# Attention and two feed-forward nets on one core: the first net's activation as one Mish instruction, weight decoding without Exp, and a planner that prices table loads

## The chip, the cores and the metric

One Trainium2 chip, one of its cores. The metric is device time in microseconds (us) of one execution; a lower one is better. Engines are named as in the profile: PE is TensorE, DVE is VectorE, ACT is ScalarE, POOL is GpSimd, SP is SyncE, whose queue issues most of the transfers.

## The reference

Three stages follow each other; inputs come as 64-bit floats.

```python
# attention: 4 batches, 8 heads, 576 positions, 64 wide
out_d  = softmax(q_d k_d^T / 8) v_d      # q_d, k_d, v_d: means over 4 neighbouring positions
local  = softmax(mask(q k^T / 8)) v      # mask: only |i - j| < 4
x = repeat(out_d, 4) + local             # [2304, 512] after joining heads
# first net, 2048 wide
h = x @ w_in
g = h * tanh(log(1 + exp(h)))            # Mish
x = g @ w_out
# second net, 1024 wide
h = x @ w3
s = h * softmax(h)
y = layernorm(s) * g_ln @ w4             # [2304, 512]
```

## The kernel before

**Work.** The 2304 tokens are 18 units of 128, in five blocks of 4, 3, 3, 4 and 4 units. `local` makes one unit's local attention: scores (line 336), Exp (line 357, or eight of them for later units), transposes (382), values (400), and the sum with the coarse part, written as two parts, high and low, into the block's x (421, 423). `coarse` makes one half of a batch's coarse attention: scores (477), six Exp with sums (491), transposes (511) with copies (514), values (525) and a copy (529). Block 0's attention comes first; that of later blocks runs between the matmuls of the first net. The tiles ku, qu and vu of later units have one buffer each.

**First net.** It runs in 80 slots, 16 for each block; the order of the segments is ten slots of block 0, sixteen of block 1, the last six of block 0, then blocks 2, 3 and 4. A slot is one chunk f of 128 of the 2048 columns of w_in for all tokens of a block (512 or 384). `chunk_in` makes h in twelve matmuls (line 632: four parts of the depth, three products of high and low parts) and then g:

```python
act: e = Exp(h)                     # line 640
dve: e = min(e, E_MAX)              # line 641
act: e = Square(e + 1)              # line 642
act: e = Ln(0.5 * e + 0.5)          # line 644
act: e = Exp(-e)                    # line 645
dve: e = (e - 1) * h                # line 646, that is -Mish(h)
act: g_high = copy(e)               # line 648
dve: g_low  = e - g_high            # line 649
```

`chunk_out` adds g's product with w_out into y (line 660, twelve matmuls), `block_end` copies y out (lines 674 on DVE, 677 on ACT) and turns the sign. h has two PSUM buffers; h is read from line 640 to line 646. The attention's tiles share the other PSUM tag, "at", with two buffers.

**Weights.** `decode` takes the bytes of the 64-bit weights apart: DVE builds the mantissa (543), ACT makes two factors from the top byte, read once as signed and once as unsigned, with Exp at a step of 16 ln 2 (545, 547), and DVE subtracts and multiplies (549, 550). `split` makes a high and a low part (553, 554).

**Second net.** `tile_in` takes 128 tokens through w3 (line 701), softmax, layer norm (Ln and Exp for the root, 742 and 743) and transposes (765); `tile_out` multiplies with w4 (782).

**Order.** Nothing runs in the order of the code. Each call of `op` puts down an engine, a cost, a wanted time ("want", in slots), its buffers and a function. `Plan.run` then plays the engines through with these costs: an engine that is free takes, of its operations that are ready and find buffers, the one with the smallest want. The order that comes out is the program. LAG is the delay that the plan adds from one engine to another; NEXT says for four slots how early and how far apart the next block's units and coarse halves are wanted; NDT, CND and CLOAD stretch the steps within them; G2LAG is the want of a tile's second product in the second net. Before the first operation, line 232 loads the table "natural_log_exp_and_others", and all Exp, Ln and Square of the kernel work with it.

Of the kernel before, what the change touches and what calls it, by code (L numbers as in the profile page):

```python
# [10 lines left out]
I32 = mybir.dt.int32  # L11
I8 = mybir.dt.int8
# [44 lines left out]


STEP = 11.090354888959125

E_MAX = 485165195.0
# [16 lines left out]
class Plan:  # L78
# [6 lines left out]
    def op(self, eng, cost, want, fn, r=(), w=(), lag=None, after=(), join=False):  # L85
# [20 lines left out]
        self.ops.append((eng, cost, want, fn, deps, list(bufs.values()), lag))  # L106
        return n

    def run(self):
# [17 lines left out]
        now, dma = 0.0, 0.0  # L127
        while len(order) < len(ops):
            for eng, queue in ready.items():
                while at[eng] <= now:  # L130
                    back, pick = [], None
                    while queue:
                        item = heapq.heappop(queue)
                        need = {}
                        for b in ops[item[1]][5]:
                            if b.tag is not None and id(b) not in held:
                                need[b.tag] = need.get(b.tag, 0) + 1
                                free.setdefault(b.tag, b.bufs)
                        if all(free[t] >= k for t, k in need.items()):
                            pick = item[1]  # L140
                            break
                        back.append(item)
                    for item in back:
                        heapq.heappush(queue, item)
                    if pick is None:
                        break
                    _, cost, _, _, _, bufs, lag = ops[pick]
# [46 lines left out]
def kernel(  # L194
# [37 lines left out]
    nc.scalar.preload_act_table_set("natural_log_exp_and_others")  # L232
# [21 lines left out]
    def act(cost, want, fn, r, w, after=()):  # L254
        return op("act", cost, want, fn, r, w, after=after)
# [31 lines left out]
    def local(u, t0, dt, gate_x=()):  # L287
# [66 lines left out]
        if u < MERGE:  # L354
            dve(dve_us(8 * KW), t0 + 0.2 * dt, lambda: nc.vector.tensor_tensor(
                heads(), heads(), nm()[:, :8].unsqueeze(2).to_broadcast([UQ, 8, KW]), op=ALU.add), [nm], [sm])
            act(act_us(8 * KW), t0 + 0.25 * dt, lambda: nc.scalar.activation(heads(), heads(), AF.Exp), [], [sm])
            dve(dve_us(8 * KW), t0 + 0.3 * dt, lambda: nc.vector.tensor_reduce(
                su()[:, :8], heads(), axis=AX.X, op=ALU.add), [sm], [su])
        else:  # L360
            for h0 in range(0, 8, 4):
                def expo(h0=h0):
                    for i in range(h0, h0 + 4):
                        nc.scalar.activation(heads()[:, i, :], heads()[:, i, :], AF.Exp, bias=nm()[:, i:i + 1],
                                             accum_out=su()[:, i:i + 1])

                act(4 * 0.32, t0 + 0.25 * dt, expo, [nm], [sm, su])
# [36 lines left out]
        passed["x", u] = pe(1.2 if early else 0.7, t0 + 0.7 * dt, values, [v, at] + ups, o + [xf], after=gate_x)  # L404
# [20 lines left out]
    def coarse(b, g2, t0, dt):  # L425
# [61 lines left out]
        for h2 in range(2):  # L487
            def expo(h2=h2):
# [5 lines left out]
            act(3 * 0.36, t0 + 0.3 * dt, expo, [nm, sc[h2]], [sm, su])  # L494
# [10 lines left out]
        for h2 in range(2):  # L505
            for k in range(2):
                tp = P("h" if early else "at")

                def flip(h2=h2, k=k, tp=tp):
                    for i in range(3):  # L510
                        nc.tensor.transpose(tp()[:72, 128 * i:128 * i + 128], sm()[:, h2, i, 72 * k:72 * k + 72], ident())  # L511

                def take(h2=h2, k=k, tp=tp):
# [3 lines left out]
                pe(0.6 if early else 0.3, t0 + 0.5 * dt, flip, [sm, ident], [tp, at])  # L517
# [15 lines left out]
    def decode(x, part, raw, n, want):  # L533
# [5 lines left out]
        plus = lambda: fb()[:, :n]  # L539
        minus = lambda: bytes_(BF16)[:, :n]  # L540
# [44 lines left out]
    g1_op = {}  # L585
    wi = {}
# [36 lines left out]
    def chunk_in(s, i, f, N):  # L623
# [4 lines left out]
        def g1():  # L628
# [24 lines left out]
    def chunk_out(s, f, fs, N, g, y):  # L653
        w = wo[f // 2]
        for d2 in range(2):
# [7 lines left out]
            pe(6 * (N + 32) / 2400, s + 1.7, g2, [w, g], [y[d2]])  # L663

    def block_end(i, s, N, y, more):
        t0 = starts[i]
        tags = (("ys", 2), ("raw", 2)) if i < NB - 1 else (("vu", 1), ("atT", 1))
        for d2 in range(2):
            ys = S([128, 2, NMAX], *tags[d2])
            for d in range(2):  # L670
                src = lambda d=d, d2=d2: y[d2]()[:, d, :N]
                dst = lambda d=d, ys=ys: ys()[:, d, :N]
                if d2:
                    dve(dve_us(N), s + 1.7, lambda src=src, dst=dst: nc.vector.tensor_scalar(
                        dst(), src(), -1.0, None, op0=ALU.mult), [y[d2]], [ys])
                else:
                    act(act_us(N), s + 1.7, lambda src=src, dst=dst: nc.scalar.activation(  # L677
                        dst(), src(), AF.Copy, scale=-1.0), [y[d2]], [ys])
# [4 lines left out]
    def tile_in(t, s):  # L683
# [11 lines left out]
        for m in range(2):  # L695
# [8 lines left out]
            pe(12 * 0.216, s, g1, [x] + [w3t[c, m][0] for c in range(4)], [hs[m if first else 0]], after=[g1_op[16 * NB - 1]] if first else ())  # L704
# [3 lines left out]
        if first:  # L708
# [5 lines left out]
            for m in range(2):  # L714
                act(act_us(512, 0.2), s + 0.2, lambda m=m: nc.scalar.activation(
                    e()[:, m], part(m), AF.Exp, bias=nm()[:, 0:1], accum_out=su()[:, 1 + m:2 + m]), [hs[m], nm], [e, su])
            dve(0.08, s + 0.3, lambda: nc.vector.tensor_tensor(
                su()[:, 0:1], su()[:, 1:2], su()[:, 2:3], op=ALU.add), [], [su])
        else:
# [3 lines left out]
                e(), hs[0](), AF.Exp, bias=nm()[:, 0:1], accum_out=su()[:, 0:1]), hs + [nm], [e, su])  # L723
# [29 lines left out]
        act(0.35, s + 0.3, root, [], [r])  # L753
# [5 lines left out]
        for m in range(2):  # L759
# [7 lines left out]
            pe(0.43, s + 0.9, flip, [e, ident], [tp])  # L767
# [6 lines left out]
    def tile_out(t, s, ln):  # L774
# [10 lines left out]
        pe(24 * 0.216, s + G2LAG, g2, [ln] + [w4t[k][0] for k in range(8)], [o])  # L785
# [13 lines left out]
    dve(0.1, -99, lambda: nc.vector.memset(ones()[:, 2:3], -64 * STEP), [], [ones])  # L799
    dve(0.1, -99, lambda: nc.vector.memset(ones()[:, 3:4], -192 * STEP), [], [ones])  # L800
# [49 lines left out]
    for k in range(8):  # L850
        second_split(k, 16 * NB - 16 + 2 * k + 2)
    for t in range(NTI):
# [72 lines left out]
```

## Time and profile before

| | |
|---|---|
| time, median of 3 runs | 742.58 us (742.24 to 742.71) |
| profiled execution, span from first to last instruction | 740.9 us |
| median less that span | 1.68 us |
| PE busy | 701.5 us, 95% |
| DVE busy | 473.3 us, 64% |
| ACT busy | 440.0 us, 59% |
| table loads | one, 1283 ns |

The page gives no other time of its own for the profiled execution than its span; the runs' times hold what lies around it as well. A busy PE counts a matmul from its start to its modelled end, and matmuls overlap, so "busy" says little on how dense the work is; the distance from one start to the next says more. The mean of 373 ns for a matmul of 512 columns on the page is such an overlapped duration.

### The profile page before, as it was taken

To read this page: it belongs to the slowest core of one execution; us is meant where nothing else is said; L and a number is where in the kernel's file an instruction comes from. 1 tells how busy PE (TensorE), PEld (TensorE's weight loads), DVE (VectorE), ACT (ScalarE), POOL (GpSimd) and SP (SyncE) were. 2 spreads that over 40 slices of the span, in tenths; PEclk is the share of its full clock that TensorE was granted. 3 is DMA by queue.
4 is the path that set the end of the run, shared out by engine and by line. 5 is a ranking of instruction groups with operands and counts; after the bars stand their busy time and mean duration, and the time that the engine had idled before them with its cause. 6 is when DMAs were issued, how large, how long until landed. Compare 5 with 4: busy or idle time off the path is not lost.

```text
span 740.9 us, 14030 instructions
## 1 busy us (share of the span) xinstructions
PE 701.5 (95%) x5720; PEld 593.3 (80%) x5720; DVE 473.3 (64%) x995; ACT 440.0 (59%) x845; POOL 33.5 (5%) x44
## 2 busy tenths in 40 slices
PE   1577999999999999999999999999999999999998
PEld 1365787899988899998888888888788888888886
DVE  4788886685854465756565545534698767667660
ACT  1458996798976677877667677756443332323321
POOL 2000101011011011000000000000000000000000
PEclk9756999999999999999999999999999999999999
DMA  8977834664353076635333123111210111010101
GB/s 240 265 264 216 248 107 96 210 146 130 114 117 85 13 162 188 161 109 179 100 112 107 63 106 116 59 56 43 82 46 30 43 42 58 30 57 29 43 28 44
DMA packets 56449, 80.48 MB, mean 109 GB/s; under 512 B 4160, under 2 KB 35392, under 8 KB 56384
## 3 DMA queue, kind: packets, MB, share of 16 engines
q1 hardware_dynamic: 52128, 72.25, 30.4%
q0 software_dynamic: 4256, 7.33, 6.2%
q8 instruction: 45, 0.74, 0.4%
q14 instruction: 20, 0.16, 0.1%
HBM read 64.88 MB, written 14.68 MB: 107 GB/s over the span
## 4 chain that ended last, share of the span: by engine, by line
PE 88%; DMA 4%; DVE 3%; ACT 3%; SPq 0%; issue 0%; DVEq 0%; ACTq 0%
PE h L632 26%; PE y L660 26%; PE at L782 13%; PE y L701 13%; DMA wo<-in_vc_dram 3%; PE at L400 3%; PE h L765 2%; PE at L336 1%; DMA wi<-in_w_dram 1%; PE at L525 1%; PE at L511 1%; PE at L382 1%; PE at L701 1%; PE at L477 1%; DMA vu<-in_vu_dram 1%; SPq L249 0%
## 5 line engine op out<-in xcount | busy, mean ns | idle before, releaser
L660 PE MATMUL y<-g,wo 128*128 128x512 f32 (+1 forms) x960 | 216.6, 373 | 0.0
L632 PE MATMUL h<-x,wi 128*128 128x512 f32 (+1 forms) x960 | 214.3, 373 | 1.2 <-DVE e L646 0.9
L632 PEld LDWEIGHTS h<-x,wi 128*128 128x128 f32 x960 | 174.4, 189 | 26.7 <-DVE e L646 2.1
L660 PEld LDWEIGHTS y<-g,wo 128*128 128x128 f32 x960 | 172.4, 188 | 23.3 <-issue 0.8
L782 PE MATMUL at<-wi,wo 128*128 128x512 f32 x432 | 102.1, 393 | 0.0
L701 PE MATMUL y<-wi,raw 128*128 128x512 f32 x408 | 96.1, 391 | 0.7 <-ACT vu L677 0.7
L782 PEld LDWEIGHTS at<-wi,wo 128*128 128x128 f32 x432 | 80.1, 188 | 16.1
L701 PEld LDWEIGHTS y<-wi,raw 128*128 128x128 f32 x408 | 76.2, 188 | 16.8 <-ACT vu L677 1.1
L646 DVE SCALAR_TENSOR_TENSOR e<-e,h 128x512 f32<-128x512 f32 (+1 forms) x80 | 50.4, 630 | 40.8 <-ACT e L645 40.0
L640 ACT ACTIVATE e<-h 128x512 f32<-128x512 f32 (+1 forms) x80 | 44.2, 553 | 52.4 <-PE h L632 51.9
L642 ACT ACTIVATE e<-e,ones 128x512 f32<-128x512 f32 (+1 forms) x80 | 54.7, 684 | 16.1 <-DVE e L641 15.4
L649 DVE TENSOR_TENSOR g<-e,g 128x512 fp32r<-128x512 f32 (+1 forms) x80 | 50.7, 634 | 18.5 <-ACT g L648 18.3
L641 DVE TENSOR_SCALAR e<-e 128x512 f32<-128x512 f32 (+1 forms) x80 | 31.8, 397 | 46.5 <-ACT e L640 46.2
L648 ACT CAST g<-e 128x512 fp32r<-128x512 f32 (+1 forms) x80 | 46.2, 578 | 24.0 <-DVE e L646 23.5
L769 ACT CAST wo<-h 128x512 fp32r<-128x512 f32 x36 | 20.7, 584 | 61.3 <-PE h L765 61.3
L644 ACT ACTIVATE e<-e,ones 128x512 f32<-128x512 f32 (+1 forms) x80 | 54.6, 682 | 1.3
L787 ACT COPY ys<-at 128x512 f32<-128x512 f32 x18 | 10.6, 587 | 63.4 <-PE at L782 63.4
L645 ACT ACTIVATE e<-e 128x512 f32<-128x512 f32 (+1 forms) x80 | 47.1, 589 | 1.3
L720 DVE TENSOR_REDUCE nm<-y 128x1 f32<-128x1024 f32 x17 | 20.8, 1224 | 25.9 <-PE y L701 25.9
L550 DVE TENSOR_TENSOR ys<-ys,f 128x512 f32<-128x512 f32 (+1 forms) x36 | 31.0, 860 | 0.3
L725 DVE TENSOR_TENSOR wo<-wo,y 128x512 f32<-128x512 f32 x34 | 23.1, 682 | 9.8 <-ACT wo L722 9.8
L770 DVE TENSOR_TENSOR wo<-h,wo 128x512 fp32r<-128x512 f32 x36 | 24.5, 683 | 4.2 <-ACT wo L769 4.1
(154 smaller groups left out, 735.1 us busy)
## 6 DMA issues: line engine op xcount, KB each, us to landing
raw<-in_w_dram SPq DMA_DIRECT2D x24, 511.6 KB
wi<-in_w_dram SPq DMA_DIRECT2D x6, 1023.2 KB
wo<-in_w_dram SPq DMA_DIRECT2D x6, 1023.2 KB
ku<-in_ku_dram SPq DMA_DIRECT2D x15, 320.0 KB
vu<-in_vu_dram SPq DMA_DIRECT2D x60, 80.0 KB
x<-in_qkc_dram SPq DMA_DIRECT2D x4, 1152.0 KB
out_dram<-ys SPq DMA_DIRECT2D x18, 256.0 KB
wscr<-ys SPq DMA_DIRECT2D x16, 256.0 KB
```

Source lines behind the costliest of these rows:

```text
L632: mm(h()[:, :N], w()[:, f % 2, a, 128 * c:128 * c + 128], x()[:, b, c, :N], start=(n == 0), stop=(n == 11))
L640: act(act_us(N), s + 0.1, lambda: nc.scalar.activation(e(), h()[:, :N], AF.Exp), [h], [eb])
L641: dve(dve_us(N, True), s + 0.1, lambda: nc.vector.tensor_scalar(e(), e(), E_MAX, None, op0=ALU.min), [], [eb])
L642: act(act_us(N, 0.09), s + 0.1, lambda: nc.scalar.activation(e(), e(), AF.Square, bias=ones()[:, 0:1]), [ones], [eb])
L644: lambda: nc.scalar.activation(e(), e(), AF.Ln, scale=0.5, bias=ones()[:, 1:2]), [ones], [eb])
L645: act(act_us(N), s + 0.1, lambda: nc.scalar.activation(e(), e(), AF.Exp, scale=-1.0), [], [eb])
L646: dve(dve_us(N), s + 0.2, lambda: nc.vector.scalar_tensor_tensor(e(), e(), 1.0, h()[:, :N], op0=ALU.subtract, op1=ALU.mult), [h], [eb])
L648: act(act_us(N), s + 0.2, lambda: nc.scalar.copy(g()[:, 0, :N], e()), [eb], [g])
L649: dve(dve_us(N), s + 0.2, lambda: nc.vector.tensor_tensor(g()[:, 1, :N], e(), g()[:, 0, :N].bitcast(F32), op=ALU.subtract), [eb], [g])
L660: mm(y[d2]()[:, d, :N], w()[:, f % 2, a, c:c + 128], g()[:, b, :N], start=(f == fs[0] and n == 0), stop=(f == fs[-1] and n == 2))
L701: mm(part(m), x()[:, a, c, :], w()[:, i, b, :], start=(n == 0), stop=(n == 11))
L782: mm(o(), ln()[:, a, k, :], w()[:, i, b, :], start=(n == 0), stop=(n == 23))
```

## The change

- `chunk_in`: lines 640 to 646 become one ScalarE instruction, Mish, that reads h and writes e. The sign that line 646 left in e is gone, so `block_end` multiplies by 1.0 in place of -1.0.
- `decode`: both Exp become Relu with a scale of 2048 and another bias, written as 16-bit integers into the same bf16 tiles, so that the bits of the power of two are made directly. Shapes and buffers stay.
- Operations can name a table. In `Plan.run` ScalarE sorts what is ready by want, plus SWITCH (1.02) if it needs another table than the loaded one; one that does costs TABLE_US (1.4) more. Exp of the attention has the table "exp", Mish "mish", the second net "ln". The table at the start is "exp_and_others"; the log table is loaded after the last Mish.
- The Exp of one unit (eight, late units) or coarse half (six) are one operation of the plan, and both transposes of one h2 in `coarse` too.
- The plan's numbers: NEXT, NDT, CND, CLOAD, G2LAG, LAG, some costs, and G2 in place of 1.7 for the want of `chunk_out`.

```diff
-NDT = 4.12
-CND = 4.5
-CLOAD = -3.17
-NEXT = {0: (0.0, 7.09, -3.0, 0.8), 26: (-2.76, 4.0, -14.0, 2.0), 32: (2.1, 10.0, 3.44, 0.94), 48: (1.51, 10.11, 4.0, 1.2)}
-G2LAG = 9.78
+NDT = 3.05
+CND = -4.17
+CLOAD = -9.08
+NEXT = {0: (-2.01, 7.12, -8.9, 2.77), 26: (-13.96, 1.33, -15.76, 5.69), 32: (-1.64, 15.27, 4.09, 3.12), 48: (-0.71, 13.65, -4.33, 12.61)}
+G2LAG = 11.09
-LAG = 0.22
+LAG = 0.16
+G2 = 2.24
+SWITCH = 1.02
+TABLE_US = 1.4
...
+                    if eng == "act":
+                        line = sorted(queue, key=lambda x: (x[0] + SWITCH * (ops[x[1]][7] not in (None, loaded)), x[1]))
...
+                    if table not in (None, loaded):
+                        loaded = table
+                        cost += TABLE_US
...
-    nc.scalar.preload_act_table_set("natural_log_exp_and_others")
+    nc.scalar.preload_act_table_set("exp_and_others")
...
-        for h2 in range(2):
-            def expo(h2=h2):
+        def expo():
+            for h2 in range(2):
...
-            act(3 * 0.36, t0 + 0.3 * dt, expo, [nm, sc[h2]], [sm, su])
+        act(6 * 0.36, t0 + 0.3 * dt, expo, [nm, *sc], [sm, su], table="exp")
...
+            pe(1.1 if early else 0.6, t0 + 0.5 * dt, flip, [sm, ident], [*tps, at])
...
-            plus(), top(I8), AF.Exp, scale=STEP, bias=ones()[:, 2:3]), [raw, ones], [fb])
+            bits(plus), top(I8), AF.Relu, scale=2048.0, bias=ones()[:, 2:3]), [raw, ones], [fb])
...
-            minus(), top(U8), AF.Exp, scale=STEP, bias=ones()[:, 3:4]), [ones], [raw])
+            bits(minus), top(U8), AF.Relu, scale=2048.0, bias=ones()[:, 3:4]), [ones], [raw])
...
-        act(act_us(N), s + 0.1, lambda: nc.scalar.activation(e(), h()[:, :N], AF.Exp), [h], [eb])
-        dve(dve_us(N, True), s + 0.1, lambda: nc.vector.tensor_scalar(e(), e(), E_MAX, None, op0=ALU.min), [], [eb])
-        act(act_us(N, 0.09), s + 0.1, lambda: nc.scalar.activation(e(), e(), AF.Square, bias=ones()[:, 0:1]), [ones], [eb])
-        act(act_us(N, 0.09), s + 0.1,
-            lambda: nc.scalar.activation(e(), e(), AF.Ln, scale=0.5, bias=ones()[:, 1:2]), [ones], [eb])
-        act(act_us(N), s + 0.1, lambda: nc.scalar.activation(e(), e(), AF.Exp, scale=-1.0), [], [eb])
-        dve(dve_us(N), s + 0.2, lambda: nc.vector.scalar_tensor_tensor(
-            e(), e(), 1.0, h()[:, :N], op0=ALU.subtract, op1=ALU.mult), [h], [eb])
+        mish_op[s] = act(act_us(N), s + 0.1, lambda: nc.scalar.activation(e(), h()[:, :N], AF.Mish), [h], [eb], table="mish")
...
-            pe(6 * (N + 32) / 2400, s + 1.7, g2, [w, g], [y[d2]])
+            pe(6 * (N + 32) / 2400, s + G2, g2, [w, g], [y[d2]])
...
+    act(0.05, 16 * NB - 0.9, lambda: nc.scalar.preload_act_table_set("natural_log_exp_and_others"), [], [], after=[mish_op[16 * NB - 1]], table="ln")
```

## Rows read from the trace of the kernel before

**Rows 1.** The page: span, and busy time of each engine with its share.

```profile
span 740.9 us, 14030 instructions
...
PE 701.5 (95%) x5720; PEld 593.3 (80%) x5720; DVE 473.3 (64%) x995; ACT 440.0 (59%) x845; POOL 33.5 (5%) x44
```

**Rows 2.** The chain that ended last: start, duration (us), what.

```profile
166.32 2.08 PE h L632 x12
...
439.35 2.72 PE h L632 x12
...
560.43 5.44 PE at L782 x24
```

**Rows 3.** Busy time by window: length, PE, PEld, DVE, ACT, POOL, clock, DMA.

```profile
65.94:136.19 70.25, 68.49 (x718) 53.90 (x718) 54.26 (x98) 57.73 (x96) 8.60 (x10) 0.98 0.50 136
136.19:420.00 283.81, 283.63 (x2876) 252.70 (x2873) 177.42 (x396) 212.82 (x419) 18.62 (x20) 1.00 0.45 126
```

**Rows 4.** The same windows for line 632 alone, then line 660: PE, PEld.

```profile
65.94:136.19 70.25, 30.93 (x119) 22.86 (x119) 0.98 0.50 136
136.19:420.00 283.81, 131.03 (x624) 110.77 (x624) 1.00 0.45 126
...
65.94:136.19 70.25, 27.44 (x108) 19.59 (x108) 0.98 0.50 136
136.19:420.00 283.81, 132.17 (x612) 107.83 (x613) 1.00 0.45 126
```

**Rows 5.** Waits of PE, 66 to 740 us: total, times, longest.

```profile
PE h L632 <- DVE e L646: 0.9, 2, 0.7
PE y L701 <- ACT vu L677: 0.7, 1, 0.7
```

**Rows 6.** Timeline, slots 0 to 3: start, duration, instructions [idle before <- releaser].

```profile
65.94 4.19 PE L632 MATMUL h<-x,wi 128*128 128x512 f32 x11 [0.24 <-DVE x L423]
...
70.06 0.97 PE L477 MATMUL at<-qkd 64*64 64x144 f32 x24
...
70.95 3.01 PE L632 MATMUL h<-x,wi 128*128 128x512 f32 x12
...
74.67 0.52 PE L511 MATMUL at<-ident,wo 128*72 128x128 f32 x3 [0.70 <-ACT wo L491]
...
75.91 3.02 PE L632 MATMUL h<-x,wi 128*128 128x512 f32 x12 [0.72 <-DVE e L646]
...
84.28 3.02 PE L632 MATMUL h<-x,wi 128*128 128x512 f32 x12
```

**Rows 7.** The page's costliest groups: count, busy us, mean ns, idle before.

```profile
L646 DVE SCALAR_TENSOR_TENSOR e<-e,h 128x512 f32<-128x512 f32 (+1 forms) x80 | 50.4, 630 | 40.8 <-ACT e L645 40.0
L640 ACT ACTIVATE e<-h 128x512 f32<-128x512 f32 (+1 forms) x80 | 44.2, 553 | 52.4 <-PE h L632 51.9
L642 ACT ACTIVATE e<-e,ones 128x512 f32<-128x512 f32 (+1 forms) x80 | 54.7, 684 | 16.1 <-DVE e L641 15.4
...
L641 DVE TENSOR_SCALAR e<-e 128x512 f32<-128x512 f32 (+1 forms) x80 | 31.8, 397 | 46.5 <-ACT e L640 46.2
...
L644 ACT ACTIVATE e<-e,ones 128x512 f32<-128x512 f32 (+1 forms) x80 | 54.6, 682 | 1.3
...
L645 ACT ACTIVATE e<-e 128x512 f32<-128x512 f32 (+1 forms) x80 | 47.1, 589 | 1.3
```

**Rows 8.** Groups by line and shape: a decode activation, and the table load.

```profile
L545 ACT ACTIVATE f<-raw,ones 128x512 bf16<-128x512 int8 x24 | 18.1, 754 | 0.0
...
L232 ACT ACT_TABLE_LOAD x1 | 1.3, 1283 | 0.7 <-PEq L910 0.7
```

**Rows 9.** Timeline of block 1's last units: SP's vu loads, then PE's values.

```profile
116.86 3.75 SPq L249 DMA_DIRECT2D vu<-in_vu_dram  x4
...
125.23 10.46 SPq L249 DMA_DIRECT2D vu<-in_vu_dram  x8
...
131.28 1.14 PE L400 MATMUL at<-wo,vu 40*64 40x32 f32 x64
```

More of the change, by code (lines that the diff above doesn't have):

```diff
@@ L11 @@
 I32 = mybir.dt.int32
+I16 = mybir.dt.int16
 I8 = mybir.dt.int8
@@ L83, in __init__, with op @@
         self.ops = []
-    def op(self, eng, cost, want, fn, r=(), w=(), lag=None, after=(), join=False):
+    def op(self, eng, cost, want, fn, r=(), w=(), table=None, after=(), join=False):
         lag = LAG
@@ L105, in op @@
                 b.readers.append(n)
-        self.ops.append((eng, cost, want, fn, deps, list(bufs.values()), lag))
+        self.ops.append((eng, cost, want, fn, deps, list(bufs.values()), lag, table))
         return n
@@ L144, in run @@
                         heapq.heappush(queue, item)
+                    if line is not None:
+                        heapq.heapify(queue)
                     if pick is None:
                         break
-                    _, cost, _, _, _, bufs, lag = ops[pick]
+                    _, cost, _, _, _, bufs, lag, table = ops[pick]
+                    if table not in (None, loaded):
+                        loaded = table
+                        cost += TABLE_US
                     for b in bufs:
@@ L356, in local @@
                 heads(), heads(), nm()[:, :8].unsqueeze(2).to_broadcast([UQ, 8, KW]), op=ALU.add), [nm], [sm])
-            act(act_us(8 * KW), t0 + 0.25 * dt, lambda: nc.scalar.activation(heads(), heads(), AF.Exp), [], [sm])
+            act(act_us(8 * KW), t0 + 0.25 * dt, lambda: nc.scalar.activation(heads(), heads(), AF.Exp), [], [sm], table="exp")
             dve(dve_us(8 * KW), t0 + 0.3 * dt, lambda: nc.vector.tensor_reduce(
@@ L360, in local @@
         else:
[L361 to L367, printed above, removed]
+            def expo():
+                for i in range(8):
+                    nc.scalar.activation(heads()[:, i, :], heads()[:, i, :], AF.Exp, bias=nm()[:, i:i + 1],
+                                         accum_out=su()[:, i:i + 1])
+            act(8 * 0.32, t0 + 0.25 * dt, expo, [nm], [sm, su], table="exp")
         def norm_a():
@@ L401, in values @@
                                at()[r, 2 * h2 + a, GQ * g:GQ * g + GQ], start=True, stop=True)
-        passed["x", u] = pe(1.2 if early else 0.7, t0 + 0.7 * dt, values, [v, at] + ups, o + [xf], after=gate_x)
+        passed["x", u] = pe(1.2 if early else 1.1, t0 + 0.7 * dt, values, [v, at] + ups, o + [xf], after=gate_x)
         for par in range(2):
@@ L505, in coarse, with flip @@
         for h2 in range(2):
-            for k in range(2):
-                tp = P("h" if early else "at")
-                def flip(h2=h2, k=k, tp=tp):
+            tps = [P("h" if early else "at") for _ in range(2)]
+            def flip(h2=h2, tps=tps):
+                for k, tp in enumerate(tps):
                     for i in range(3):
                         nc.tensor.transpose(tp()[:72, 128 * i:128 * i + 128], sm()[:, h2, i, 72 * k:72 * k + 72], ident())
+            pe(1.1 if early else 0.6, t0 + 0.5 * dt, flip, [sm, ident], [*tps, at])
+            for k, tp in enumerate(tps):
                 def take(h2=h2, k=k, tp=tp):
@@ L585 @@
     g1_op = {}
+    mish_op = {}
     wi = {}
@@ L702, in g1 @@
                         n += 1
-            pe(12 * 0.216, s, g1, [x] + [w3t[c, m][0] for c in range(4)], [hs[m if first else 0]], after=[g1_op[16 * NB - 1]] if first else ())
+            pe(12 * 0.227, s, g1, [x] + [w3t[c, m][0] for c in range(4)], [hs[m if first else 0]], after=[g1_op[16 * NB - 1]] if first else ())
         nm = S([128, 3], "nm2", 2)
@@ L715, in tile_in @@
                 act(act_us(512, 0.2), s + 0.2, lambda m=m: nc.scalar.activation(
-                    e()[:, m], part(m), AF.Exp, bias=nm()[:, 0:1], accum_out=su()[:, 1 + m:2 + m]), [hs[m], nm], [e, su])
+                    e()[:, m], part(m), AF.Exp, bias=nm()[:, 0:1], accum_out=su()[:, 1 + m:2 + m]), [hs[m], nm], [e, su], table="ln")
             dve(0.08, s + 0.3, lambda: nc.vector.tensor_tensor(
@@ L722, in tile_in @@
             act(act_us(1024, 0.2), s + 0.2, lambda: nc.scalar.activation(
-                e(), hs[0](), AF.Exp, bias=nm()[:, 0:1], accum_out=su()[:, 0:1]), hs + [nm], [e, su])
+                e(), hs[0](), AF.Exp, bias=nm()[:, 0:1], accum_out=su()[:, 0:1]), hs + [nm], [e, su], table="ln")
         for m in range(2):
@@ L783, in g2 @@
                     n += 1
-        pe(24 * 0.216, s + G2LAG, g2, [ln] + [w4t[k][0] for k in range(8)], [o])
+        pe(24 * 0.227, s + G2LAG, g2, [ln] + [w4t[k][0] for k in range(8)], [o])
         os_ = S([128, 512], "ys", 2)
```

30 lines of the change are left out of this document (18 added, 12 removed).

## The prediction

> **What bounds the kernel now.** I read the page first [rows 1]. The span is 740.9 us, the runs shown have a median of 742.58, so 1.68 us lie around the span; I sum against the span and add that again. TensorE is busy for 95% of it, ScalarE for 59%, VectorE for 64%. A busy TensorE can still be slow, so next I read the chain of waits, for the pace at which TensorE cannot go faster [rows 2]: twelve matmuls of 512 columns take 2.72 us in the first net, 24 take 5.44 in the second net, so 0.2267 each; twelve of 384 columns take 2.08, so 0.1733 each. From about 420 us on the chain is such pieces back to back. There a lighter ScalarE can give nothing.
>
> So the question is what idle time TensorE has before that. I cut the trace in windows: from the first dense run of slot 0 (65.94) to slot 10, the first chunk of block 1 (136.19), and from there to 420 [rows 3], and asked the same windows for lines 632 and 660 alone [rows 4]. In the first, 119 + 108 dense matmuls at 0.2267 need 51.5 us; what is left of the weight-load time, 53.90 - 22.86 - 19.59 = 11.45, I take as the price of the attention's small matmuls. Together 62.9 of 70.25 us: 7.3 idle. Part of it is the clock: the first eleven matmuls lie between 65.94 and 70.06, 4.12 us where 2.49 would do, 1.6 lost [rows 6]. The mean granted clock of this window is 0.98, of the later ones 1.00 [rows 3]. Nothing in the change touches that, and 5.7 remain. In the second window 32 of the slots are blocks 1 and 2 (384 columns, 768 matmuls, 133.1 us), the other 468 matmuls need 106.1, attention 252.70 - 110.77 - 107.83 = 34.1: 273.3 of 283.8, 10.5 idle. The waits of TensorE between 66 and 740 us say what can be named of it [rows 5]: 0.9 us on line 646, the last operation that reads h, and 0.7 us at the junction of the nets, on ScalarE's line 677. The rest is short: pieces of time lost when TensorE goes from large matmuls to small ones and back, which have no releaser.
>
> The timeline shows the wait on line 646 at its worst [rows 6]. Slot 1's twelve matmuls start at 70.95 and would end at 73.67. Slot 2 starts at 75.91, released by line 646, which gives slot 0's h back. Between lie 2.24 us with one group of three transposes in it, 0.52, so 1.7 idle. Slot 3 waits for slot 1's h until 84.28. There are two h buffers, and each is held through six instructions in a ScalarE queue that also decodes weights.
>
> **The activation.** Six instructions become one. By the page's groups [rows 7], lines 642, 644 and 645 take 54.7 + 54.6 + 47.1 = 156.4 us from ScalarE, and lines 641 and 646 take 31.8 + 50.4 = 82.2 us from VectorE. Line 640, 44.2 us, stays with another function. No row shows Mish. I price it at line 640's 0.553 mean, which reads the same h without a bias pointer; the dearest group here, line 642 at 0.684, is the upper bound, line 645 at 0.589 is between. The difference of 0.13 per chunk is hidden by the slots of 4.2 to 5.4 us. The h buffer is now free after one instruction.
>
> **The table loads.** Exp, and Mish beside it, are taken to need different tables. After slot 0 there are 14 local units and 5 coarse halves with Exp: 19 batches, at most 38 switches and one for the second net, half of that if pairs are merged. The one load shown takes 1.283 us [rows 8], so 25 to 50 us of ScalarE; the net is still 106 to 131 us less. In the first window it is closer: ten chunks give back at least 10 x 156.4/80 = 19.6, and the three units of block 1 and a coarse half can ask for eight loads, 10.3. ScalarE goes from 57.73 to about 48.5 of 70.25 us, VectorE from 54.26 by 10 x 82.2/80 to 44.0. Beyond the load I add nothing for a switch, since the row shows only the load; it is the first ScalarE instruction, so it can't show what a switch in mid-flow costs, and I keep the upper end open as a rival.
>
> That row is 1.283 us and no more. The Trainium skill, page ScalarE: Activation LUTs, section What ACT_TABLE_LOAD costs, has the same load and about 1.38 us of drain behind it, 2.66 for every switch; by that the eight would be an estimated 21.3 us and ScalarE would be no emptier in this window than before. No run here shows that yet.
>
> **The decode.** Two Exp with a bias pointer on one byte in eight become two Relu of the same form that write int16. The 512-column form takes 0.754 us [rows 8]. Below, a plain activation of this width has line 640's price, 0.55, so up to 0.2 per instruction could be gained; above, no row prices the conversion to int16, and I allow the same 0.2 as loss. I take 0: the read pattern and the pointer stay. The first decodes lie in the start, where four pairs of them are near the chain, so the range gets plus or minus 1.6 us for it. That they need no Exp is what keeps them out of the switches.
>
> **The planner.** NEXT, NDT, CND and CLOAD bring the attention of the next block about two slots forward; G2 goes from 1.7 to 2.24, so the first matmul of the slot after next goes ahead of g2 when its h is free; an Exp that needs a load is sorted 1.02 slots later. Joined Exp of a coarse half hold both score banks until the sixth has run, and a joined flip wants two "at" banks at once: at most one copy later for each half, off the dense path. The start up to slot 0 keeps its constants for loads and weights, so I move it by 0, with plus or minus 2 us because another order comes out of the costs. The second net keeps its work; G2LAG only moves each tile's second product further back, and it has nothing to win. There the new load of the log tables stands right behind the last Mish, before the copy of the last g: 1.283 us, covered by the second net's first matmuls that the planner already mixes in.
>
> **Where the stall goes.** With h free early, TensorE runs on to the next thing that is late. That is slot 10's x. Block 1's units share one vu buffer: its four loads are issued at 116.86 and 125.23, the last values run at 131.28, and slot 10 starts at 136.19 [rows 9]. If TensorE comes early it has one group of second products (2.72 us) to put ahead, so 2.7 us are covered even if this chain keeps its place.
>
> **The sum.** First window: the 1.7 us and a third of the other 4.0, 1.3, since ScalarE and VectorE are lighter there: -3.0. Second window: a quarter of 10.5, -2.6, because hardly any of it has a releaser. Junction: -0.2 of 0.7, because line 677 stays and only what is queued before it gets shorter. Start, decode, second net: 0. Total -5.8: span 735.1, time 736.8 us.
>
> **The rivals.** (A, forecast) Stalls on h go, the switches fit in ScalarE's idle time: 736.8, its own range 733.5 to 739.5. Chance 0.45. (B) The start or the attention gets a better order too, and the idle time of both windows goes for the most part: 5.7 + 6 + 0.7 = 12.4 less, 730.2. For it: 16.2 us idle in all before 420. Against: the idle time that has no releaser. Chance 0.20. (C) The vu chain keeps its place and g of slot 9 is not ready as cover: the first window gives nothing, 742.6 - 2.8 = 739.8. For it: its loads wait for each other through one buffer. Against: its start moves with TensorE's order. Chance 0.15. (D) A switch costs more than its load, so that eight of them eat the 19.6 us: that is from 2.45 us each on. Then ScalarE is as full as before, slots 2 and 3 wait on as now, and little is left, 742.0. Chance 0.08. It is also where the change would not do what it says, if the planner's price merged nothing. It is the case in which the Trainium skill's rule above (ScalarE: Activation LUTs, What ACT_TABLE_LOAD costs) would decide. (E, the other sign) The switches lie bare on block 1's attention: each of its four Exp batches comes a load to and a load back later, 4 x 2.57 = 10.3 us, and slot 10 slips by that less the cover of 2.7, so 7.6 late, against 2.8 gained elsewhere: 742.6 + 4.8 = 747.4. It decides from 5.5 us of slip on, over half of the eight loads. For it: single buffers and an in-order queue make that attention serial. Against: it is started two slots earlier, and ScalarE has 21.8 us idle in that window. Chance 0.12.
>
> **The numbers.** 0.2%, 1.5 us, is about what this kernel's runs can tell from no change. Faster: A, B and C less the upper tails, 0.75; within 0.2%: D and those tails, 0.13; slower: E, 0.12. The range leaves out E and the lower tail of B, under 2 in 10: 729 to 743.
>
> **What will show it.** Mish at about 0.55 to 0.60 us; 20 to 40 loads of 1.283 us; ScalarE near 310 to 335 us and VectorE near 391; slot 2 following slot 1 without a gap; slot 10 before 134 us; from there to the second net hardly closer. Wrong would be: a first dense run more than 2 us away from 65.94 (B or worse), slot 10 later than 136 with TensorE waiting on line 423 (E), or idle time behind every load that is longer than the load (D).

## The result, and the profile after

| | before | after |
|---|---|---|
| time, median of 4 runs each | 742.41 us (741.90 to 742.71) | 736.13 us (734.62 to 737.12) |
| span of the profiled execution | 740.9 us | 735.0 us |
| ratio of the times, 95% interval | | 0.9914 (0.9899 to 0.9930) |

The forecast was 736.8 us. The profiled execution is 5.9 us shorter, and its page begins so:

```profile
span 735.0 us, 13720 instructions
...
PE 701.1 (95%) x5720; PEld 596.5 (81%) x5720; DVE 402.4 (55%) x835; ACT 350.5 (48%) x641; POOL 33.4 (5%) x44
```

TensorE does the same work in the same busy time [rows 1]; ScalarE and VectorE lost 89.5 and 70.9 us. ScalarE's groups by line and shape (count | busy us, mean ns of one | idle before) show the new instruction, the loads and the decode:

```profile
L655 ACT ACTIVATE e<-h 128x512 f32<-128x512 f32 x48 | 28.7, 598 | 100.5 <-PE h L647 100.4
L655 ACT ACT_TABLE_LOAD x18 | 23.1, 1283 | 0.3
...
L559 ACT ACTIVATE f<-raw,ones 128x512 int16<-128x512 int8 x24 | 18.1, 756 | 0.0
...
L370 ACT ACT_TABLE_LOAD x13 | 16.7, 1283 | 0.2
...
L503 ACT ACT_TABLE_LOAD x4 | 5.1, 1283 | 1.1 <-DVE cnm L498 1.0
```

One Mish of 512 columns takes 0.598 us, and it waits for h alone. There are 35 loads among the work of the first net, at lines 655, 370 and 503, each of 1.283 us as the one load of before [rows 8]. All 18 units take a single Exp (line 370), so the joined Exp are those of the coarse halves alone. A decode with Relu takes 0.756 us where the one with Exp took 0.754.

The two windows of rows 3, from slot 0's first product to slot 10 and from there to 415.49, first all engines (length, PE, PEld, DVE, ACT, POOL, clock, DMA), then line 647 (h) and line 668 (y) alone:

```profile
63.91:135.18 71.27, 71.27 (x680) 57.03 (x677) 51.01 (x86) 55.19 (x92) 8.31 (x9) 1.00 0.52 149
135.18:415.49 280.31, 280.31 (x2861) 250.83 (x2860) 134.92 (x289) 167.25 (x294) 17.96 (x20) 1.00 0.46 129
...
63.91:135.18 71.27, 31.37 (x121) 23.61 (x121) 1.00 0.52 149
135.18:415.49 280.31, 131.67 (x624) 110.93 (x624) 1.00 0.46 129
...
63.91:135.18 71.27, 30.05 (x120) 21.78 (x120) 1.00 0.52 149
135.18:415.49 280.31, 127.93 (x601) 105.93 (x600) 1.00 0.46 129
```

The second window ends at 415.49, where slot 62 begins: the products of h are done for 62 slots there, the second products for 60 (one of each is counted on both sides of an edge). Before, the same work was done at 420.15, so 4.7 of the 5.9 us are won by that point. TensorE's timeline shows where the first of them lie (start, duration, instructions):

```profile
63.91 7.59 PE L647 MATMUL h<-x,wi 128*128 128x512 f32 x24
71.43 0.78 PE L349 MATMUL at<-ku,qu 64*32 64x40 f32 x64
72.14 3.06 PE L647 MATMUL h<-x,wi 128*128 128x512 f32 x12
...
78.43 2.89 PE L647 MATMUL h<-x,wi 128*128 128x512 f32 x12
...
87.14 3.02 PE L647 MATMUL h<-x,wi 128*128 128x512 f32 x12
...
130.14 1.14 PE L412 MATMUL at<-wo,vu 40*64 40x32 f32 x64
131.21 1.65 PE L668 MATMUL y<-g,wo 128*128 128x512 f32 x6
132.79 0.97 PE L489 MATMUL at<-qkd 64*64 64x144 f32 x24
133.69 1.66 PE L668 MATMUL y<-g,wo 128*128 128x512 f32 x6
135.18 4.35 PE L647 MATMUL h<-x,wi 128*128 128x384 f32 x24
...
518.85 5.60 PE L668 MATMUL y<-g,wo 128*128 128x512 f32 x24
524.29 5.73 PE L709 MATMUL y<-wi,raw 128*128 128x512 f32 x24
```

Slots 0 and 1 run as one stretch, slot 2 begins at 72.14 behind one attention group, slot 3 at 78.43. In rows 6 they began at 75.91 and 84.28, and slot 2 waited for line 646. Of TensorE's waits between 66 and 740 us [rows 5] the trace of the changed kernel names none. Slot 10 is only 1.01 us earlier than in rows 4, but more is done by then. Now the twelve matmuls of line 668 between the last values of block 1 (130.14) and slot 10 are the last second products of slot 9. Before, twelve of line 660 stood at that place too, and twelve more of block 0 were still to come behind slot 10's first two groups:

```profile
140.46 2.92 PE L660 MATMUL y<-g,wo 128*128 128x512 f32 x12
...
420.15 2.88 PE L660 MATMUL y<-g,wo 128*128 128x512 f32 x12
```

At the junction of the nets 518.85 + 24 x 0.2267 = 524.29: line 709 follows without the 0.7 us of rows 5.

### The profile page after: what moved, and what is told of

The parts are those of the page before. It is cut to its first block, busy times and chain, and to the rows that moved or that the text cites. A ratio compares the mean times of both kernels' runs of the same rounds, so it can differ in the third digit from the quotient of the medians.

```text
span 735.0 us, 13720 instructions
## 1 busy us (share of the span) xinstructions
PE 701.1 (95%) x5720; PEld 596.5 (81%) x5720; DVE 402.4 (55%) x835; ACT 350.5 (48%) x641; POOL 33.4 (5%) x44
## 4 chain that ended last, share of the span: by engine, by line
PE 92%; DMA 4%; DVE 2%; ACT 1%; issue 1%; SPq 0%; DVEq 0%; ACTq 0%
PE h L647 28%; PE y L668 27%; PE at L790 13%; PE y L709 13%; PE at L412 3%; DMA wo<-in_vc_dram 3%; PE h L773 2%; PE at L349 1%; PE at L523 1%; DMA wi<-in_w_dram 1%; PE at L538 1%; PE at L489 1%; PE at L394 1%; PE at L709 1%; DVE e L422 0%
## 5 line engine op out<-in xcount | busy, mean ns | idle before, releaser
L561 ACT ACTIVATE raw<-raw,ones 128x512 int16<-128x512 uint8 x24 | 18.1, 755 | 11.3 <-DVE ys L557 10.5
L655 ACT ACT_TABLE_LOAD x18 | 23.1, 1283 | 0.3
L739 DVE BATCH_NORM_STATS2 bs<-wo 128x6 f32<-128x512 f32 x36 | 23.0, 683 | 0.0
L260 POOL DMA_DIRECT2D vd<-in_vc_dram x18 | 15.9, 882 | 157.4 <-PE h L647 57.5
L568 DVE TENSOR_TENSOR wi<-ys,wi 128x1024 fp32r<-128x1024 f32 x16 | 19.6, 1225 | 5.4 <-ACT wi L567 5.3
```

Of the source, the lines that this page charges most:

```text
L655: mish_op[s] = act(act_us(N), s + 0.1, lambda: nc.scalar.activation(e(), h()[:, :N], AF.Mish), [h], [eb], table="mish")
L739: dve(dve_us(512), s + 0.3, lambda m=m: nc.vector.bn_stats(bs()[:, m, :], e()[:, m, :]), [e], [bs])
```

## Experiments

Theory: h comes free after one instruction, which takes the stalls of the first slots away; the loads lie in ScalarE's idle time; the decode changes no time but saves loads. Rivals: the new numbers of the planner bring the gain, whatever the activation; the loads cost something that is hidden in the sum; the attention of block 1 becomes late (E). Diffs are against the changed kernel where nothing else is said; each ratio compares runs on one chip. Slots begin with their first matmul of h.

**1. The old activation in the new plan.**

```diff
-nc.scalar.activation(e(), h()[:, :N], AF.Mish)   # table="mish"
+# the six instructions of lines 640 to 646, with E_MAX and the sign
-nc.scalar.preload_act_table_set("exp_and_others")
+nc.scalar.preload_act_table_set("natural_log_exp_and_others")
```

> The changed kernel with the six-instruction activation put back (one table for all, so no loads in mid-flow); decode with Relu and all numbers of the planner stay as changed. Theory A (the time came from the h buffer that is free after one instruction): the stall of slots 1 to 3 is back, 1.7 to 3 us before slot 4, and the time is 740 to 744 us. Theory B (the planner's new numbers gave a better order, the activation little): 736 to 738 us.

Measured: 768.19 us, ratio 1.0334 (1.0298 to 1.0370). That is outside both ranges. The new numbers alone are no gain: with the old chain they cost 25 us, and slot 10 starts at 154.15. So these numbers gain nothing without Mish. Whether numbers sought for the old chain would, no run asks.

**2. Mish with the planner's old numbers.**

```diff
-NDT, CND, CLOAD = 3.05, -4.17, -9.08
+NDT, CND, CLOAD = 4.12, 4.5, -3.17
-NEXT = {0: (-2.01, 7.12, -8.9, 2.77), 26: ...}
+NEXT = {0: (0.0, 7.09, -3.0, 0.8), 26: ...}      # all as before
-G2LAG, LAG, G2 = 11.09, 0.16, 2.24
+G2LAG, LAG, G2 = 9.78, 0.22, 1.7
```

> The changed kernel with Mish, Relu decode and priced loads, but NEXT, NDT, CND, CLOAD, G2, G2LAG and LAG as before. Theory A: TensorE's loss between 66 and 85 us stays small, 736 to 739 us. Theory B: most of the gain is lost, 740 to 744 us.

Measured: 752.08 us, 1.0125 (1.0100 to 1.0150), outside both ranges too. Mish alone is no gain either. TensorE's timeline ahead of slot 10 shows why [in brackets: idle before, and its releaser]:

```profile
131.38 0.97 PE L489 MATMUL at<-qkd 64*64 64x144 f32 x24
135.76 0.38 PE L412 MATMUL at<-wo,vu 40*64 40x32 f32 x4 [3.41 <-ACT raw L503]
136.84 1.92 PE L412 MATMUL at<-wo,vu 40*64 40x32 f32 x60 [0.71 <-ACT raw L503]
...
149.97 5.28 PE L647 MATMUL h<-x,wi 128*128 128x384 f32 x21
```

The coarse scores of the next batch (L489) come ahead of the values of unit 5 (L412) and take both "at" banks. The values wait 3.41 us, until the third of the joined Exp (L503) gives a bank back, and 0.71 more for the other, after the sixth. The products of slots 0 to 9 are all done by then, so all that is left of block 1 is done in a row, with nothing dense between, and slot 10 begins at 149.97. In before and in the changed kernel the scores come after the last values (135.30 against 131.28, and 132.79 against 130.14 above). The windows of this stretch add the clock's part (seventh value after the length):

```profile
129.00:135.90 6.90, 3.49 (x99) 2.55 (x98) 5.19 (x13) 4.23 (x12) 0.82 (x1) 1.00 0.80 211
135.90:142.70 6.80, 5.71 (x80) 4.44 (x78) 2.94 (x7) 3.15 (x11) 0.89 (x1) 0.50 0.72 199
...
146.10:152.90 6.80, 6.25 (x89) 5.60 (x90) 2.82 (x7) 2.30 (x3) 0.84 (x1) 0.50 0.73 150
```

After 3.41 us without work TensorE is granted 0.50, the 1.2 GHz level, for 6.8 us, and again from 146.10, so slot 10 itself begins at half pace.

Runs 1 and 2 also make a square with the two kernels, and it tells which part of the change does what:

| | activation, plan's numbers | slot 0 to slot 4, us | second products done in them | TensorE's wait at the junction |
|---|---|---|---|---|
| before | six instructions, old | 64.92 to 90.47: 25.55 | 24 | 0.7 us |
| run 1 | six instructions, new | 64.20 to 90.91: 26.71 | 24 | none |
| run 2 | Mish, old | 64.84 to 88.71: 23.87 | 36 | 0.7 us |
| changed | Mish, new | 63.91 to 87.14: 23.23 | 30 | none |

```profile
64.92 0.78 PE L632 MATMUL h<-x,wi 128*128 128x512 f32 x1
...
90.47 2.99 PE L632 MATMUL h<-x,wi 128*128 128x512 f32 x12
```

```profile
64.20 7.68 PE L650 MATMUL h<-x,wi 128*128 128x512 f32 x24
...
90.91 3.02 PE L650 MATMUL h<-x,wi 128*128 128x512 f32 x12
```

```profile
64.84 7.01 PE L647 MATMUL h<-x,wi 128*128 128x512 f32 x24
...
88.71 5.60 PE L647 MATMUL h<-x,wi 128*128 128x512 f32 x24
...
539.63 5.74 PE L709 MATMUL y<-wi,raw 128*128 128x512 f32 x24 [0.71 <-ACT vu L685]
```

With Mish the first slots are shorter and hold more second products (six are 1.36 us) under either set of numbers; without it they are not, under either. The attention groups in between differ by one or two of about 1 us, so tenths mean nothing here. The wait at the junction is gone with the new numbers, under either activation.

**3. Relu for Mish, same order, no loads.** This shows what the loads cost.

```diff
-nc.scalar.activation(e(), h()[:, :N], AF.Mish)
+nc.scalar.activation(e(), h()[:, :N], AF.Relu)
```

> The changed kernel with Relu where Mish stands, so the first net's activation is another function; the order of the plan is the same, and all 35 table loads in mid-flow are gone (two remain, at the start and before the second net). Theory A (the loads lie in idle time of ScalarE): ScalarE is 45 us less busy and the time is 734 to 737 us, within 0.3% of the changed kernel. Theory C (the loads lie partly bare on attention or h): 728 to 733 us, with slot 10 and the later blocks earlier.

Measured: 736.60 us, 0.9914 (0.9890 to 0.9937), the same ratio as the changed kernel. Its page has ScalarE 45.8 us less busy than the changed kernel's:

```profile
PE 699.8 (95%) x5720; PEld 595.7 (81%) x5720; DVE 401.8 (55%) x835; ACT 304.7 (42%) x606; POOL 32.6 (4%) x44
```

35 instructions and 35 x 1.283 = 44.9 us fewer, and no time won. The two traces hold the same 5720 matmuls in the same order, so they can be laid side by side:

```profile
63.14 6.46 PE L647 MATMUL h<-x,wi 128*128 128x512 f32 x24
...
133.19 4.35 PE L647 MATMUL h<-x,wi 128*128 128x384 f32 x24
```

Slot 1 begins 1.90 us earlier than in the changed kernel (66.71 against 68.61), ahead of the first load in mid-flow, because this execution started earlier and its clock rose at 64.7 in place of 67.9. Slot 10 is 1.99 us earlier, slot 62 (413.47) 2.02. So by these two traces all 35 loads together cost about 0.1 us in this order.

**4. Loads without a price in the plan.**

```diff
-SWITCH = 1.02
-TABLE_US = 1.4
+SWITCH = 0.0
+TABLE_US = 0.0
```

> The changed kernel with a planner that puts no price on a table load (SWITCH and TABLE_US are 0); the program has 33 loads in place of 37, so the prices did not thin them out. Theory A: another order of the same work, 735 to 738 us. Theory C (the prices are what keeps the loads off the path): 739 us or more, with TensorE waiting behind loads before slot 10.

Measured: 751.61 us, 1.0110 (1.0086 to 1.0133). There are not more loads but fewer, 31 in place of 35. So the price does not save loads; it changes the order. The time lies in the range of theory C, but its cause is not seen: without the price the scores stand at 129.79, the values of unit 5 wait behind them until 134.60, slot 10 begins at 147.85.

**5. The old numbers, with the new NEXT of slot 0 and the new steps.** Run 2 with two of its edits taken back.

```diff
 # against run 2
-NEXT = {0: (0.0, 7.09, -3.0, 0.8), 26: ...}
+NEXT = {0: (-2.01, 7.12, -8.9, 2.77), 26: ...}   # 26, 32 and 48 stay old
-NDT, CND, CLOAD = 4.12, 4.5, -3.17
+NDT, CND, CLOAD = 3.05, -4.17, -9.08
```

> The kernel with Mish and the old numbers of the planner (752 us, slot 10 at 149.97), with NEXT for slot 0, NDT, CND and CLOAD as changed; NEXT for slots 26, 32 and 48, G2, G2LAG and LAG stay as before. Theory D (those 9 us lie in when block 1's attention is done, and nowhere else): slot 10 comes before 138 us and the time is 735 to 739 us. Theory E (the other numbers carry it, or any order differs by this much): slot 10 stays later than 142 us and the time above 742 us.

Measured: 758.71 us, 1.0211 (1.0185 to 1.0238). Slot 10 comes 5.1 us earlier than in run 2 (144.91), but another hole opens ahead of slot 48, which begins at 356.24, against 332.56 in the changed kernel. There TensorE waits 4.30 and 2.13 us for line 386, the local softmax on VectorE, and no scores of line 489 are in it. Placing one block earlier moves the loss to another; half of the numbers is no half of the gain.

**6. The decode with Exp again.**

```diff
-bits(plus), top(I8), AF.Relu, scale=2048.0, ...
+plus(), top(I8), AF.Exp, scale=STEP, ...   # table="exp"; minus likewise
```

> The changed kernel with the decode's Relu turned back to Exp, priced as such: 83 loads in place of 37, 59 us more of ScalarE, most of them before 160 us. Theory A (ScalarE's idle time takes loads): 736 to 740 us. Theory C (where ScalarE is full, loads lie bare): slot 10 later than 140 us, 743 to 760 us; the decode without Exp is then what makes the change possible.

Measured: 762.18 us, 1.0259 (1.0238 to 1.0281). That is above the range of theory C. Beside the first load there are 82: 41 at Mish, 33 at the decode itself (27 at line 562, 6 at 564), 6 at the local Exp and two single ones. The order is another one too (slot 10 at 153.47), so the 26 us are not the price of 46 loads alone. One piece can be told: from 160 to 212 us ScalarE is busy for 48.28 of 52 us, 18 loads (23.1 us) among it, and then TensorE waits for weights that ScalarE splits too late:

```profile
218.13 1.01 PE L671 MATMUL y<-g,wo 128*128 128x384 f32 x2 [6.78 <-ACT wo L570]
```

**7. The old LAG alone.**

```diff
-LAG = 0.16
+LAG = 0.22
```

> The changed kernel with LAG alone as before (0.22 in place of 0.16): a small step of one planner number, 35 loads. If the gain is robust against such a step: 734.5 to 738 us. If the order that came out happens to fit: more than 3 us away, with slot 10 later than 138 us.

Measured: 747.97 us, 1.0067 (1.0045 to 1.0089), with 33 loads in the first net. A planning delay of 0.06 us costs 12 us: the values of unit 5 wait 1.24 us for their vu transfer, the scores (132.42) pass those of unit 6 (138.79), slot 10 begins at 141.61, 6.4 us late. That is half of the loss: slot 48 begins at 346.71, 14.2 us late, behind a wait of 2.62 us for line 422, a sum on VectorE.

**8. A second buffer for unit 5's values.** Against rival C's chain through the one vu buffer.

```diff
-*(("g", 3) if other else ("vu", 1))
+*(("g", 3) if other else ("atT", 1) if u == 5 else ("vu", 1))
...
-after=gate + [passed.get(("x", u - 1))] * (not early)   # the loads wait for these values
+after=gate + [passed.get(("x", u - 2 if u in (5, 6) else u - 1))] * (not early)
```

> The changed kernel, but block 1's middle unit has its values loaded into the tile atT, which is free then, so its loads do not wait for the first unit's values. Theory F (the row of vu loads holds slot 10): the values of block 1's units follow each other in 3 to 5 us in place of 7.7, slot 10 starts at 130 to 132 us in place of 135.2, and the time is 732.5 to 735 us. Rival (TensorE's own work reaches slot 10 no earlier, or the loads are late by the first unit's coarse part): slot 10 within 1 us of 135 and 735 to 737 us.

Measured: 746.15 us, 1.0053 (1.0034 to 1.0071), outside both ranges. The values of units 4 and 5 are now 2.66 us apart (126.39 and 129.05) where they were 7.70 apart, but the whole chain moves back: the second coarse half's values come at 121.43 in place of 110.26, the scores again ahead of unit 6's values, slot 10 at 143.04. The longest wait there, 2.87 us, is not for a bank: it ends on line 386, unit 6's softmax on VectorE. The spacing by the buffer was real, and not what decides.

**9. Mish in the order of before.** The plan still counts the six old instructions, only Mish is issued, at the place of the first; decode with Relu.

```diff
 # against before
-act(..., AF.Exp), [h], [eb])
+act(..., mish, [h], [eb])
+# the other five keep cost and place in the plan and issue nothing
```

> The kernel before with its order of instructions kept: the planner still plans six instructions, but only Mish is issued at the place of the first (the other five issue nothing), decode uses Relu, and 41 loads, which no price has placed, come where that order needs them. TensorE's order is the one of before. Theory A (the early h buffer is worth the time by itself): TensorE's loss falls by 2 to 3 us between 66 and 85, slot 10 stays at 134 to 136.5 us, and the time is 737.5 to 740.5 us. Theory B (only another order gains): 741.5 to 743.5. Theory C (loads that no price placed lie bare): over 743.5 us.

Measured: 752.21 us, 1.0124 (1.0105 to 1.0142), with 41 loads in the first net where no place was planned for them. TensorE's two longest waits:

```profile
77.18 0.52 PE L512 MATMUL at<-ident,wo 128*72 128x128 f32 x3 [1.88 <-ACT wo L492]
77.46 4.59 PE L634 MATMUL h<-x,wi 128*128 128x512 f32 x12
...
284.25 0.26 PE L337 MATMUL at<-ku,qu 64*32 64x40 f32 x2 [1.82 <-ACT raw L492]
```

Each of them ends on coarse Exp with a load right ahead of these (74.64 to 75.92, 281.71 to 282.99), and each is followed by 3.4 us at the lower clock (0.50, from 77.72 and from 285.93). By these chains loads do cost here; this order was not run without loads, so the rest of its 9.5 us is open. The run also shows what the early h buffer gives by itself, for TensorE's matmuls stand in the order of before: slot 2 now begins 0.28 us after the transposes (77.18 to 77.46), where it began 1.24 us after them (74.67 to 75.91) [rows 6]. The stall on h was 0.96 us.

**10. Only the decode.**

```diff
 # against before
-plus(), top(I8), AF.Exp, scale=STEP, ...
+bits(plus), top(I8), AF.Relu, scale=2048.0, ...   # minus likewise
```

> The kernel before with the decode alone changed to Relu; the planner's costs and its order are the same, one table. Every theory: decode instructions of 0.755 and 1.24 us as before, the time within 1 us of before. More than 1.5 us away would be a price of the int16 output.

Measured: 741.95 us, 1.0002 (0.9985 to 1.0019). In the same order and with one table the Relu decode costs nothing and gives nothing.

**11. Run 2 without loads.** Relu for Mish, in run 2's order.

```diff
 # against run 2
-nc.scalar.activation(e(), h()[:, :N], AF.Mish)
+nc.scalar.activation(e(), h()[:, :N], AF.Relu)
```

> The kernel with Mish and the planner's old numbers (752 us), with Relu in place of Mish so that the 35 loads in mid-flow are gone and the order stays the same; the activation is another function. Theory C (the loads make block 1's attention late in that order): slot 10 near 140 us or earlier in place of 150, 738 to 743 us. Theory G (the order alone, with the chain of vd loads behind the first coarse half, makes it late): slot 10 at 147 to 150 us and 749 to 752 us.

Measured: 751.79 us, 1.0130 (1.0112 to 1.0147), against 1.0125 with the loads. Its timeline has the same hole:

```profile
133.63 0.42 PE L412 MATMUL at<-wo,vu 40*64 40x32 f32 x4 [3.41 <-ACT raw L503]
...
148.41 6.81 PE L647 MATMUL h<-x,wi 128*128 128x384 f32 x24
```

The loss of run 2 is its order, not its loads.

**12. Block 1's coarse values from a buffer of their own.** If slot 10's x bounds the changed kernel, an earlier x is a gain.

```diff
-v = vb = S([72, 2, 2, 128], "vd", 1)
+v = vb = S([72, 2, 2, 128], *(("atT", 1) if (b, g2) == (1, 1) else ("vd", 1)))
```

> The changed kernel, with the vd of block 1's second coarse half in the tile atT, which is free then, so that its four loads need not wait for the first half's values. Theory G (the chain of vd loads sets when block 1's attention is done): the second half's values at 90 to 100 us in place of 110.3, slot 10 at 125 to 132 us, and 731 to 735 us. Rival (vu's loads or TensorE's own work come next, or the new order loses elsewhere): slot 10 at 133 us or later and 735.5 us or more.

Measured: 737.30 us, 0.9929 (0.9914 to 0.9943); the interval overlaps that of the changed kernel. The second half's values come at 105.50, later than forecast. The timeline around slot 10:

```profile
132.02 2.27 PE L647 MATMUL h<-x,wi 128*128 128x384 f32 x12
...
137.30 2.92 PE L668 MATMUL y<-g,wo 128*128 128x512 f32 x12
```

Slot 10 begins 3.2 us earlier, and its twelve second products of slot 9 simply come after it, at 137.30. The end does not move: there TensorE's own work is the bound, as the changed kernel's list of waits, empty after 66 us, says. No run here beats the changed kernel.

## Why the prediction came out right, step by step

**First window, forecast -3.0, measured -2.9.** From slot 0's first product to slot 10 both kernels take 71.27 us (64.92 to 136.19, 63.91 to 135.18). By the working of the prediction the changed kernel does 240 dense matmuls in them (the 121st of line 647 is slot 10's first) x 0.2267 = 54.4, and attention 57.03 - 23.61 - 21.78 = 11.6, so 5.2 us are idle. Before, with the one matmul at 64.92, it was 228 x 0.2267 = 51.7 and 11.45, so 8.1. The clock is no part of the gain: of the idle time the lower clock has 2.1 now and 1.6 then. Slots 0 and 1 take 7.52 us up to the next start where 24 x 0.2267 = 5.44 would do. (The clock column says 1.00 because the first clock record of this trace lies behind them, at 67.9; the matmuls start 0.427 us apart up to there, and 0.227 from there on.)

**The stall of 1.7 us on h.** The wait on line 646 is gone as forecast, and by the table under run 2 the gain of the first slots comes with Mish. But the size was read too high. Rows 6 have two waits in these 1.7 us: 0.72 on line 646, and 0.70 on ScalarE's coarse Exp (line 491). Run 9 gets 0.96 back at this place. Slot 3's 84.28 was no wait at all: TensorE had other work right up to it. So about 1 us is the stall itself, and the rest of the first window comes from the order that the plan makes when it counts h as free early.

**Where the stall went.** Slot 10's x was named as the next late thing, with one group of second products as cover. The cover was used: this window holds 240 dense matmuls, not 227. So rival C, in which slot 9's g is not ready as cover, fell. The expected sign "slot 10 before 134" was wrong by 1.2 us, and was a poor sign: in run 12 slot 10 begins at 132.02 with no gain. It is the count of products done that tells.

**Second window, forecast -2.6, measured -0.9.** 768 x 0.1733 = 133.1, 457 x 0.2267 = 103.6, attention 250.83 - 110.93 - 105.93 = 34.0, so 9.6 of 280.31 are idle, against 10.5. The term was mis-sized: I took a quarter of idle time that has no releaser, though I had said that hardly any of it can be named. Not a quarter of it came but a tenth.

**Start, forecast 0 within 2, measured -1.0.** Slot 0's first product moved from 64.92 to 63.91; by the first dense stretch it is 65.94 to 63.91, just over the 2 us that I gave as a sign of B, but one of its matmuls ran ahead then. In run 3, the same order, it is at 63.14, so executions of one order differ by nearly as much as this gain, and no run shows that it is the change's.

**Junction, forecast -0.2, measured -0.9.** The wait on line 677 is gone altogether:

```profile
526.62 2.88 PE L660 MATMUL y<-g,wo 128*128 128x512 f32 x12
530.21 8.46 PE L701 MATMUL y<-wi,raw 128*128 128x512 f32 x36 [0.71 <-ACT vu L677]
```

526.62 + 12 x 0.2267 = 529.34, so 0.87 was lost. The forecast's reason, less work queued ahead of line 677, was wrong: by the table under run 2 the wait stays with Mish under the old numbers and is gone with the new ones.

**The sum.** Ahead of the junction before had 0.4 more that I forecast as 0: from 420.15 to 529.34 it takes 109.19 us for 480 dense matmuls, the changed kernel 108.80, which is 480 x 0.2267. In all -1.0 - 2.9 - 0.9 - 0.4 - 0.9 = -6.1, of which rounding and the price of attention take 0.2; behind the junction nothing is won. So 736.8 was met by errors that cancel, and that is luck: the windows were forecast 0.1 and 1.7 too well, the start, the end of the first net and the junction 1.0, 0.4 and 0.7 too badly. Of the 5.9 us the square gives some 2 to 3 to Mish and 0.9 to the numbers. The start, the second window and the 0.4 are not given to either.

**Loads, rival D.** Forecast 20 to 40, measured 35 in the first net, 1.283 each. ScalarE's timeline at the first switch:

```profile
69.12 0.23 ACT L503 ACTIVATION_READ_ACCUMULATOR wo<-at,cnm 128x1 f32 x1
69.37 1.28 ACT L655 ACT_TABLE_LOAD   x1
70.66 0.60 ACT L655 ACTIVATE e<-h 128x512 f32<-128x512 f32 x1
71.54 0.60 ACT L655 ACTIVATE e<-h 128x512 f32<-128x512 f32 x1 [0.28 <-PE h L647]
72.03 1.14 ACT L656 CAST g<-e 128x512 fp32r<-128x512 f32 x2
```

69.12 + 0.23 = 69.35, the load at 69.37, its end at 70.65, Mish at 70.66: 0.01 to 0.02 us on either side. At 23 of the 35 loads the next instruction follows within 0.012 us. Nothing lies behind the load, so D falls. The Trainium skill, page ScalarE: Activation LUTs, section What ACT_TABLE_LOAD costs, has a drain of about 1.38 us with each; the load agrees with its 1.28, no row here shows the drain, and the measurement decides.

**The decode, forecast 0,** is 0 by run 10; what it does is keep loads away (run 6).

**Busy time of the engines.** Mish at 0.555 us in the mean of both widths is as forecast. ScalarE was forecast near 310 to 335 and has 350.5: 440.0 - 156.4 + 36 x 1.283 = 329.8 counts each removed instruction at its full mean, but neighbours overlap (71.54 + 0.60 ends 0.11 us after the next start). The durations of all ScalarE instructions sum to 54.8 us more than its busy time before and to 33.7 more after, and the difference, 21.1, is what the forecast has too much. Over 240 removed instructions the 20.7 us are 0.086 each. VectorE likewise: 402.4, not 391, 0.07 for each of 160. Neither is the bound.

**Rival E** was not what happened here, but late attention of block 1 is real next door: slot 10 is 6 to 15 us late in runs 2, 4, 7 and 8, which take 752, 752, 748 and 746 us; the forecast was 747.4. In run 7 half of the loss lies elsewhere, so that price was met by chance there. Its cause as I put it, loads bare on block 1's attention, is wrong for run 2: run 11 loses the same without a load. What the four share is that the scores of the next batch pass unit 6's values and that TensorE has done all products of slots 0 to 9 by the time it meets block 1's last pieces. In runs 2 and 4 it then waits for the "at" banks that the scores hold; in runs 7 and 8 the longest waits end on a copy, a transfer and VectorE's softmax. In run 2 the clock falls behind the hole. The prediction had joined Exp "off the dense path"; that is true only in orders in which the scores come last. I had no row that could have told which order the plan would give.

## What to carry to other kernels

A lighter activation pays where a buffer that TensorE waits for is held through its chain, and there by the stall that a row names; read in that row what each piece of the stall waits for. Idle time without a releaser gave a tenth of itself here. When work orders itself by a plan, neither the operation nor the plan's numbers need have a gain of its own (752 and 768 us alone, 736 together), so change and retune together, and look for the late piece that a new order lets pass. Such a time belongs to one order out of many: each edit of the plan's numbers, buffers or decode in runs 4, 6, 7, 8 and 12 left it the same or made it worse, by up to 26 us, and how far a search for the old chain would have come is untested. Table loads were free in the two orders that were run with and without them (runs 2 and 11, and the changed kernel and run 3); where ScalarE was full (run 6) or no place was planned (run 9), TensorE waited behind them. To see their price, run a function of the same cost that needs no load, in the same order.

## What the hardware showed that I had not expected

- Table loads in mid-flow take 1.283 us with 0.01 to 0.02 us to their neighbours, so a switch is the load and no more.
- Mish from PSUM costs what Exp did: 0.555 us in the mean of both widths, against 0.553 of line 640 [rows 7].
- One hole of 3.41 us in TensorE's work is followed by 6.8 us at the lower clock level (0.50) in run 2, though TensorE is busy for 5.71 of those 6.8 us.
- ScalarE's neighbours overlap by some 0.09 us, so sums of means say too much of what a removed instruction frees.
